# Transposes on TensorE in place of DMA transposes, and another order in the short chunks, in a one-core adaLN block with local attention and a gated MLP

## The chip, the cores and the metric

The kernel runs on one core of one Trainium2 chip. The metric is the device time of one execution in microseconds (us). "Before" is the median of three runs of the unchanged kernel; one execution of it was profiled.

## What is computed

The block takes 2048 tokens of 576 features in bf16. `mod` is six vectors of 576, made from a condition `c`.

```python
sa, ca, ga, sb, cb, gb = silu(c) @ w_mod          # six vectors of 576
h = layernorm(x) * (1 + ca) + sa                  # LN1 and its modulation
q, k, v = split(h @ wqkv)                         # 32 heads of 18 features
# each token attends to 8 tokens: itself and those 2, 4, ... 14 positions back
o = softmax(q . k_window / sqrt(18)) @ v_window
x = x + ga * (o @ wo)
h = layernorm(x) * (1 + cb) + sb                  # LN2 and its modulation
x = x + gb * (((h @ w_gate) * (h @ w_up)) @ w_down)   # 4608 hidden features
```

## The kernel before

**Chunks and passes.** The tokens are cut into ten chunks (`SIZES`): chunks 0 to 3 have 128 tokens ("short"), chunks 4 to 9 have 256. The MLP runs in seven passes over the weights: passes 0 to 3 take one short chunk each, pass 4 takes chunks 4 and 5 together, pass 5 takes 6 and 7, pass 6 takes 8 and 9. In a pass `gate_up` multiplies the normalized tokens with blocks of gate and up weights (L667 for the first 512 features, L676 for the last 64); ScalarE (ACT) copies the result out of PSUM (L684), and VectorE (DVE) multiplies gate by up (L685). After every 512 tokens `down` multiplies by `w_down` (L715) and writes the rows out. Gate and up weights come in blocks by DMA, during pass 0 from the queue of GpSimd (POOL), later from SyncE's (SP).

**Attention beside the MLP.** While the MLP of one pass runs, the attention of the next pass's chunks is prepared. `project(ci)` does LN1 of a chunk (`ln_rows`), turns the rows into feature-major form `hT`, and multiplies for q and k (L480), their last 64 features (`qkr`, L487) and v (L505). The v rows go to a buffer in DRAM (`vd`, L512), from which `vsh`, the windows of v, are read back (L522). `attend(ci)` forms the logits (L548), the softmax on DVE and ACT, the weighted sum over `vsh` (L606 to L609) that gives `o_sb`, turns that into `oT`, multiplies by `wo` (L623), adds to x, does LN2 into `o_sb`, and turns that into `h2T`, the input of the chunk's MLP pass.

**Order.** These two generators stop at labels (`hT`, `q0`, `v0`, `oT`, `wo0`, `h2T` and so on). `period(ci)` merges `project(ci + 1)` and `attend(ci)` by a table that gives each label a place between 0 and 1 in the period of the chunk, and `Pacer` lets a step go as the emitted MLP matmuls reach that place. There are three tables: `AT_SHORT` for chunks of 128, `AT_FIRST` for chunks 4 and 5, and `AT` for chunks 6 to 9. So the order of TensorE's (PE's) instructions is largely fixed by the tables. In passes 0 to 3 a scheduler also moves them; from pass 4 PE's order is as emitted. The setup before pass 0 is written out by hand.

**Turning.** Five feature tiles cover 576 features. The fifth has only 64, and they are wanted twice, on partitions 0 to 63 and again on 64 to 127, since L676 uses both halves of the array. So the rows `xn` and `o_sb` are 640 wide (`DP`), and `ln_rows` writes features 512 to 575 a second time into columns 576 to 639 (the second round of the loop at L385; ACT at L390 or DVE at L388). `turn` (L403 to L410) makes five 128x128 transposes on PE for each 128 tokens into two PSUM banks, and ACT and DVE bring them back with the modulation (`modulate`, L429 and L431), or ACT copies them for `oT` (L616, L617). For the chunks in `BY_DMA` (`hT` of 7, 8, 9; `oT` of 6 to 9; `h2T` of 4 and 6 to 9) `turn_by_dma` writes the rows to DRAM and reads them back with a DMA transpose, both from SP's queue (L414, L415), and POOL modulates in place (L420).

```python
        for m in range(n):
            for j in range(C // P):
                nc.tensor.transpose(banks[b][:, m, j * P:(j + 1) * P], src[:, j, (m0 + m) * P:(m0 + m + 1) * P], ident)
```

Of the kernel before, what the change touches and what calls it, by code (L numbers as in the profile page):

```python
# [16 lines left out]

P = 128
D = 576
DP = 640  # L20
KT = 5
H = 32
DH = 18
# [26 lines left out]
LOAD_X = {3: [6]}  # L50
LOAD_X_DOWN = {0: [7, 8], 1: [9]}

BY_DMA = dict(hT={7, 8, 9}, oT={6, 7, 8, 9}, h2T={4, 6, 7, 8, 9})

AT = dict(lg0=.06, lg1=.14, lgT=.19, hT=.31, q0=.37, q1=.41, k0=.45, k1=.49, qkr=.52, v0=.55, v1=.58,
          ws=.60, oT=.61, wo0=.66, wo1=.70, h2T=.86)

AT_FIRST = dict(AT, hT=.24, q0=.29, q1=.34, k0=.39, k1=.44, qkr=.48, v0=.52, v1=.57, ws=.64, oT=.66, wo0=.70, wo1=.74, h2T=.92)

AT_SHORT = dict(AT_FIRST, oT=.55, wo0=.60, h2T=.80)  # L60


@with_exitstack
def kernel(
# [41 lines left out]
    def hp():  # L106
        return tc.high_priority()
# [27 lines left out]
    xn = once.tile([P, CH // P, DP], BF, name="xn")  # L135
# [4 lines left out]
    o_sb = once.tile([P, CH // P, DP], BF, name="o_sb")  # L140
    oT = once.tile([P, KT, CH], BF, name="oT")
    vd = dramp.tile([HALO + S, D], BF, name="vd")
    turned = {k: dramp.tile([CH, DP], BF, name=f"{k}_d") for k in ("xn1", "o", "xn2")}

    nc.scalar.preload_act_table_set("natural_log_exp_and_others")

# [38 lines left out]
    nc.vector.memset(o_sb[:, :, D:], 0.0)  # L185

    def wm_tile():
        return sp.tile([P, KT, 2 * D], BF, name="wm", bufs=2)
# [175 lines left out]
    def ln_rows(src, into, j0=0, dve=False):  # L364

        ST = len(src)

        st = small.tile([P, CH // P, 14], F32, name="ln_stats", bufs=1)
        stats, mv = st[:, :, 0:12].rearrange("p j (a b) -> p j a b", a=2), st[:, :, 12:14]
        for j in range(ST):  # L370
            for hf in range(2):
                nc.vector.bn_stats(stats[:, j, hf, :], src[j][:, hf * 288:(hf + 1) * 288])  # L372
            nc.vector.bn_aggr(mv[:, j, :], stats[:, j, :, :].rearrange("p a b -> p (a b)"))
        rstd = small.tile([P, CH // P], F32, name="ln_rstd")
        nc.vector.tensor_scalar_add(rstd[:, 0:ST], mv[:, 0:ST, 1], EPS)  # L375
        nc.vector.tensor_scalar_mul(mv[:, 0:ST, 0], mv[:, 0:ST, 0], -1.0)
        yield
        nc.scalar.activation(rstd[:, 0:ST], rstd[:, 0:ST], ACTF.Ln)  # L378
        nc.scalar.activation(rstd[:, 0:ST], rstd[:, 0:ST], ACTF.Exp, scale=-0.5)
        if not dve:  # L380
            nmr = small.tile([P, CH // P], F32, name="ln_nmr")
            for j in range(ST):
                nc.scalar.activation(nmr[:, j:j + 1], mv[:, j, 0:1], ACTF.Identity, scale=rstd[:, j:j + 1])  # L383
        yield
        for d0, s0 in ((slice(0, D), 0), (slice(D, DP), D - 64)):  # L385
            for j in range(ST):
                if dve:
                    nc.vector.tensor_scalar(into[:, j0 + j, d0], src[j][:, s0:D], mv[:, j, 0:1], rstd[:, j:j + 1], ALU.add, ALU.mult)  # L388
                else:
                    nc.scalar.activation(into[:, j0 + j, d0], src[j][:, s0:], ACTF.Identity, bias=nmr[:, j:j + 1], scale=rstd[:, j:j + 1])  # L390

    def banks2(early, dt, name):

# [9 lines left out]
    def turn(src, C, early=False):  # L403

        banks = [b[:, 0:n * C].rearrange("p (m c) -> p m c", c=C) for b, n in zip(banks2(early, BF, "turn"), (3, 2))]
        for b, m0, n in ((0, 0, 3), (1, 3, 2)):
            for m in range(n):
                for j in range(C // P):
                    nc.tensor.transpose(banks[b][:, m, j * P:(j + 1) * P], src[:, j, (m0 + m) * P:(m0 + m + 1) * P], ident)
# [27 lines left out]
    def project(ci):  # L437
# [4 lines left out]
        for _ in ln_rows(x_tiles[ci], xn, j0):  # L442
            if ci == 1:
                yield "ln"
        h = hT[:, :, j0 * P:j0 * P + C]
        if ci in BY_DMA["hT"]:
            turn_by_dma(h, xn, "xn1")
            yield "hT"
            modulate_in_place(h, 0)
        else:  # L450
            yield "hT"
            banks = turn(xn[:, j0:, :], C, early=ci == 1)
            if ci < 2:
                yield "hTe"
            modulate(h, banks, 0, act_only=ci == 1)
# [68 lines left out]
    def attend(ci, dst):  # L524
# [76 lines left out]
        else:  # L601
            for j in range(ST):
# [10 lines left out]
            if ci not in BY_DMA["oT"]:  # L613
                banks = turn(o_sb, C)
        if ci not in BY_DMA["oT"]:
            (nc.vector.tensor_copy if ci == 0 else nc.scalar.copy)(oT[:, 0:3, 0:C], banks[0])  # L616
            nc.scalar.copy(oT[:, 3:5, 0:C], banks[1])  # L617
        for j in range(ST):
            yield f"wo{j}"
            pw = banks2(ci == 0, F32, "pw")  # L620
# [11 lines left out]

        for _ in ln_rows(x_t, o_sb, dve=ci == 0):
            pass
        if ci in BY_DMA["h2T"]:
            turn_by_dma(dst, o_sb, "xn2")
        yield "h2T"
        if ci in BY_DMA["h2T"]:
            modulate_in_place(dst, 2)
        else:  # L640
            modulate(dst, turn(o_sb, C), 2)

    def gate_up(pi, c0, C, h2, step):

# [4 lines left out]
        cs = slice(c0, c0 + C)  # L649
        ns = C / 2.4  # L650

        def tokens(rows, kt):
            return h2[rows, :, kt, :] if C > CH else h2[rows, c0 // CH, kt, c0 % CH:c0 % CH + C]

        def by_half(ap):
            return ap.rearrange("p (a c) -> p a c", c=CH) if C > CH else ap


        nf = 2 if C <= 256 else 1
        units = [(b, i) for b in ORDER[pi] for i in range(0, FB, nf)]  # L660
# [1 line left out]
        def main(u, first):  # L662
            (b, i), out = units[u], ps[u]
            for n in range(nf):
                for t in range(2):
                    for kt in range(KT - 1):
                        nc.tensor.matmul(by_half(out[:, t, n, 0:C]), lhsT=gu_blocks[b][0][:, kt, t, (i + n) * P:(i + n + 1) * P], rhs=tokens(slice(0, P), kt),  # L667
                                         start=(first and n == 0 and kt == 0), stop=(not first and kt == KT - 2), skip_group_check=True)
                step(8 * ns)

        def rem(u, first):
            (b, i), out = units[u], ps[u]
            for n in range(nf):
                for t in range(2):
                    rows = slice(64 * t, 64 * (t + 1))
                    nc.tensor.matmul(by_half(out[:, t, n, 0:C]), lhsT=gu_blocks[b][1][rows, (i + n) * P:(i + n + 1) * P], rhs=tokens(rows, KT - 1),  # L676
                                     start=(first and n == 0), stop=not first, skip_group_check=True)

        def evacuate(u):
# [52 lines left out]
    def attend_into_place(ci):  # L732
        di, c0 = home[ci]
        if di not in h2T:
            h2T[di] = h2p.tile([P, CM // CH, KT, CH], BF, name="h2T")
        return attend(ci, h2T[di][:, c0 // CH, :, c0 % CH:c0 % CH + SIZES[ci]])

    def period(ci):

        gens = {"a": project(ci + 1)} if ci + 1 < NCH else {}  # L740
        gens["b"] = attend_into_place(ci)
        at = AT_SHORT if SIZES[ci] == P else AT_FIRST if ci < 6 else AT
        nxt = {k: next(g) for k, g in gens.items()}
        while nxt:
            k = min(nxt, key=lambda k: at[nxt[k]])
            yield at[nxt[k]]
            nxt[k] = next(gens[k], None)
            if nxt[k] is None:
                del nxt[k]
# [121 lines left out]
```

## Time and profile before

| | |
|---|---|
| median of 3 runs | 582.46 us (582.19 to 582.83) |
| profiled execution, its own time | 582.19 us |
| its span | 580.5 us |
| PE busy | 564.4 us (97%), 5171 matmuls |
| DVE busy | 309.0 us (53%) |
| ACT busy | 258.6 us (45%) |
| POOL busy | 92.5 us (16%) |
| granted PE clock | 1.0 throughout |
| DMA | 84.33 MB, mean 145 GB/s |

The span runs from the first to the last instruction; the execution's own time is 1.7 us longer. A matmul's time in the profile (219 ns for one with 128 columns) holds its way through the array; how many of them PE does in a stretch is read from their starts.

### The profile page before, as it was taken

How to read it: one execution, taken by the hardware profiler on the slowest of the kernel's cores; microseconds unless marked ns; L12 is line 12 of the kernel's file. 1: busy time of each engine (PE TensorE's matmuls, PEld its weight loads, DVE VectorE, ACT ScalarE, POOL GpSimd, SP SyncE). 2: the span in 40 equal slices, each digit the busy share in tenths (PEclk: the TensorE clock that was granted, in tenths of full speed). 3: DMA queues.
4: the chain of work that ended last, by engine and by line, in shares of the span. 5: the costliest groups of instructions: out<-in, count | busy, mean ns of one | idle time of the engine just before them, and what ended most of it. 6: DMA issues, size and time to landing. Idle time of an engine off the chain costs nothing.

```text
span 580.5 us, 12340 instructions
## 1 busy us (share of the span) xinstructions
PE 564.4 (97%) x5171; PEld 368.8 (64%) x5171; DVE 309.0 (53%) x687; ACT 258.6 (45%) x475; POOL 92.5 (16%) x165
## 2 busy tenths in 40 slices
PE   7999999999999999999999999999999999999996
PEld 4577888878878764554458774554457754444675
DVE  5777686857868765845376525844374412222101
ACT  3465667575552245456542225455440225454200
POOL 4553201021113112011400231011200020000000
PEclk9999999999999999999999999999999999999999
DMA  8999763458751254477502542486302214550000
GB/s 291 273 355 341 251 201 115 134 184 269 248 184 44 75 189 113 127 245 218 136 1 77 194 103 93 118 251 219 95 1 56 67 39 144 155 163 1 1 21 20
DMA packets 68458, 84.33 MB, mean 145 GB/s; under 512 B 19618, under 2 KB 59506, under 8 KB 68402
## 3 DMA queue, kind: packets, MB, share of 16 engines
q1 hardware_dynamic: 56738, 45.86, 27.3%
q0 software_dynamic: 9104, 34.44, 17.9%
q10 hardware_dynamic: 2560, 3.25, 1.6%
q8 instruction: 40, 0.66, 0.5%
q14 instruction: 16, 0.13, 0.1%
HBM read 70.93 MB, written 8.67 MB: 137 GB/s over the span
## 4 chain that ended last, share of the span: by engine, by line
PE 79%; DMA 8%; ACT 5%; DVE 4%; issue 2%; POOL 1%; SPq 0%; ACTq 0%; POOLq 0%
PE pgu L667 38%; PE acc L715 22%; PE pgu L676 6%; PE pq L480 5%; DMA vd<-v_sb 3%; PE lgT L548 2%; DMA wd<-in_B_w_up_dram 2%; ACT gu L684 2%; DMA wqk<-in_A_wqkv_dram 2%; DMA wv<-in_A_wqkv_dram 2%; PE pwB L623 1%; PE pwA L623 1%; PE pvB L505 1%; PE pvA L505 1%; ACT o_sb L390 1%
## 5 line engine op out<-in xcount | busy, mean ns | idle before, releaser
L667 PE MATMUL pgu<-h2T,gm 128*128 128x512 bf16 (+1 forms) x1504 | 239.0, 311 | 0.6 <-ACT gu L684 0.3
L684 ACT CAST gu<-pgu 128x1024 bf16<-128x1024 f32 (+1 forms) x180 | 145.2, 843 | 122.2 <-PE pgu L676 97.7
L667 PEld LDWEIGHTS <-gm 128*128 128x128 bf16 x1504 | 118.4, 98 | 107.7 <-issue 15.7
L715 PE MATMUL acc<-wd,hh 128*128 128x288 bf16 x1152 | 146.5, 286 | 0.5 <-DVE y L721 0.5
L685 DVE TENSOR_TENSOR hh<-gu 128x512 bf16<-128x512 bf16 (+1 forms) x180 | 66.2, 371 | 144.9 <-ACT gu L684 144.0
L715 PEld LDWEIGHTS <-hh 128*128 128x128 bf16 x1152 | 112.3, 98 | 29.5 <-issue 1.2
L539 DVE TENSOR_TENSOR prod<-qT,kT 128x1280 bf16<-128x1280 bf16 (+1 forms) x80 | 46.8, 637 | 13.5 <-PE lgT L548 12.4
L522 POOL DMA_DIRECT2D vsh<-vd x30 | 22.6, 756 | 153.4 <-DMA vd<-v_sb 89.1
L721 DVE TENSOR_TENSOR y<-acc,gb_bc 128x576 bf16<-128x576 f32 (+1 forms) x17 | 12.3, 721 | 57.9 <-PE acc L715 57.9
L480 PE MATMUL pq<-hT,wqk 128*128 128x256 bf16 (+1 forms) x400 | 41.2, 251 | 0.8 <-DMA wqk<-in_A_wqkv_dram 0.8
L724 POOL DMA_DIRECT2D out_dram<-y x15 | 8.5, 566 | 208.1 <-DVE y L723 208.1
L606 DVE TENSOR_TENSOR vsh<-vsh,attn 128x2304 bf16<-128x2304 bf16 x30 | 39.9, 1351 | 0.2
L676 PE MATMUL pgu<-h2T,gr 64*128 64x512 bf16 (+1 forms) x376 | 37.0, 311 | 0.0
L480 PEld LDWEIGHTS <-wqk 128*128 128x128 bf16 x400 | 32.3, 98 | 6.8 <-DMA wqk<-in_A_wqkv_dram 1.5
L667 PE MATMUL pgu<-h2T,wd 128*128 128x128 bf16 x512 | 34.7, 219 | 1.4 <-DMA wd<-in_B_w_gate_dram 0.6
L667 PEld LDWEIGHTS <-wd 128*128 128x128 bf16 x512 | 30.4, 98 | 3.0 <-DMA wd<-in_B_w_up_dram 0.9
L372 DVE BATCH_NORM_STATS2 ln_stats<-x_t 128x6 f32<-128x288 bf16 x64 | 26.5, 447 | 7.4 <-ACT ln_nmr L383 5.3
L378 ACT ACTIVATE ln_rstd<-ln_rstd 128x2 f32<-128x2 f32 (+1 forms) x20 | 4.1, 203 | 53.5 <-DVE ln_rstd L375 53.4
L676 PEld LDWEIGHTS <-gr 64*128 64x128 bf16 x376 | 12.2, 94 | 18.9 <-issue 12.3
L420 POOL TENSOR_SCALAR h2T<-h2T,modc 128x256 bf16<-128x256 bf16 x25 | 14.7, 598 | 38.0 <-DMA h2T<-xn_d 38.0
L607 DVE TENSOR_TENSOR vsh<-vsh 128x2304 bf16<-128x2304 bf16 x15 | 20.2, 1349 | 0.0
L482 ACT CAST qT<-pq 128x512 bf16<-128x512 f32 (+1 forms) x20 | 10.1, 504 | 21.9 <-PE pq L480 21.9
(146 smaller groups left out, 483.3 us busy)
## 6 DMA issues: line engine op xcount, KB each, us to landing
vsh<-vd POOLq DMA_DIRECT2D x30, 576.0 KB, 6.3
gm<-in_B_w_gate_dram SPq DMA_DIRECT2D x24, 512.0 KB, 4.1
gm<-in_B_w_up_dram SPq DMA_DIRECT2D x24, 512.0 KB, 5.4
wd<-in_B_w_down_dram SPq DMA_DIRECT2D x4, 1152.0 KB, 7.0
gm<-in_B_w_gate_dram POOLq DMA_DIRECT2D x5, 512.0 KB, 11.7
gm<-in_B_w_up_dram POOLq DMA_DIRECT2D x5, 512.0 KB, 11.5
out_dram<-y POOLq DMA_DIRECT2D x15, 144.0 KB, 2.1
wd<-in_B_w_gate_dram POOLq DMA_DIRECT2D x4, 512.0 KB, 10.0
```

The costliest lines, as they stand in the source:

```text
L372: nc.vector.bn_stats(stats[:, j, hf, :], src[j][:, hf * 288:(hf + 1) * 288])
L420: nc.gpsimd.tensor_scalar(dst[:, m, :], dst[:, m, :], modc[:, vi + 1, m:m + 1], modc[:, vi, m:m + 1], ALU.mult, ALU.add)
L480: nc.tensor.matmul(pq[:, gi, 0:C], lhsT=wqk[:, kt, w0:w0 + P], rhs=h[:, kt, :], start=(kt == 0), stop=(kt == KT - 1))
L522: nc.gpsimd.dma_start(vsh[:].rearrange("p w d h -> p w (d h)"), src)
L539: nc.vector.tensor_tensor(prod[:, 0:nm, 0:C], qT[:, 0:nm, 0:C], kT[:, 0:nm, off:off + C], ALU.mult)
L606: nc.vector.tensor_tensor(vsh[:], vsh[:], attn[:, j, ws, None, :].to_broadcast([P, WG, DH, H]), ALU.mult)
L607: nc.vector.tensor_tensor(va[:], va[:], vb[:], ALU.add)
L667: nc.tensor.matmul(by_half(out[:, t, n, 0:C]), lhsT=gu_blocks[b][0][:, kt, t, (i + n) * P:(i + n + 1) * P], rhs=tokens(slice(0, P), kt), s ...
L676: nc.tensor.matmul(by_half(out[:, t, n, 0:C]), lhsT=gu_blocks[b][1][rows, (i + n) * P:(i + n + 1) * P], rhs=tokens(rows, KT - 1), start=(f ...
L684: nc.scalar.copy(g, ps[u][:, :, :, 0:C].rearrange("p t n c -> p n t c"))
L685: nc.vector.tensor_tensor(hh[:, fs, cs], g[:, :, 0, :], g[:, :, 1, :], ALU.mult)
L715: nc.tensor.matmul(acc[:, q, 0:288], lhsT=hh[:, f, j * P:(j + 1) * P], rhs=wd[:, f, q * 288:(q + 1) * 288], start=(f == 0), stop=(f == FT ...
```

## The change

- All chunks are turned on PE. `BY_DMA`, `turn_by_dma`, `modulate_in_place` and the three DRAM buffers go away. Twelve turns of 256 tokens are concerned: three of `hT`, four of `oT`, five of `h2T`.
- The rows are 576 wide. `ln_rows` no longer writes the last 64 features twice. `turn` makes the fifth tile of each 128 tokens by two transposes of 64 columns, one to the upper and one to the lower 64 partitions.
- `h2T` is one tile of 512 tokens in place of two halves of 256, so the matmuls of `gate_up` read their tokens as one run.
- The tables: chunks 6 to 9 now use what chunks 4 and 5 used (`hT` .24 for .31, q and k earlier by some .06 to .08, `oT` .66 for .61, `wo0` .70 for .66, `h2T` .92 for .86). For the short chunks `qkr` goes from .48 to .47, `oT` from .55 to .52, `wo0` from .60 to .59, `v0` from .52 to .66, `v1` from .57 to .72, `h2T` from .80 to .90.

```diff
-DP = 640
-BY_DMA = dict(hT={7, 8, 9}, oT={6, 7, 8, 9}, h2T={4, 6, 7, 8, 9})
-AT = dict(lg0=.06, lg1=.14, lgT=.19, hT=.31, q0=.37, q1=.41, k0=.45, k1=.49, qkr=.52, v0=.55, v1=.58,
-          ws=.60, oT=.61, wo0=.66, wo1=.70, h2T=.86)
-AT_FIRST = dict(AT, hT=.24, q0=.29, q1=.34, k0=.39, k1=.44, qkr=.48, v0=.52, v1=.57, ws=.64, oT=.66, wo0=.70, wo1=.74, h2T=.92)
-AT_SHORT = dict(AT_FIRST, oT=.55, wo0=.60, h2T=.80)
+AT = dict(lg0=.06, lg1=.14, lgT=.19, hT=.24, q0=.29, q1=.34, k0=.39, k1=.44, qkr=.48, v0=.52, v1=.57,
+          ws=.64, oT=.66, wo0=.70, wo1=.74, h2T=.92)
+AT_SHORT = dict(AT, qkr=.47, oT=.52, wo0=.59, v0=.66, v1=.72, ws=.51, h2T=.90)
...
-        for d0, s0 in ((slice(0, D), 0), (slice(D, DP), D - 64)):
-            for j in range(ST):
...
-                    nc.scalar.activation(into[:, j0 + j, d0], src[j][:, s0:], ACTF.Identity, bias=nmr[:, j:j + 1], scale=rstd[:, j:j + 1])
+        for j in range(ST):
...
+                nc.scalar.activation(into[:, j0 + j, :], src[j][:], ACTF.Identity, bias=nmr[:, j:j + 1], scale=rstd[:, j:j + 1])
...
-                    nc.tensor.transpose(banks[b][:, m, j * P:(j + 1) * P], src[:, j, (m0 + m) * P:(m0 + m + 1) * P], ident)
+                    out = banks[b][:, m, j * P:(j + 1) * P]
+                    if m0 + m < KT - 1:
+                        nc.tensor.transpose(out, src[:, j, (m0 + m) * P:(m0 + m + 1) * P], ident)
+                    else:
+                        for rows in (slice(0, 64), slice(64, P)):
+                            nc.tensor.transpose(out[rows], src[:, j, D - 64:D], ident)
...
-    def turn_by_dma(dst, src, key):
-        nc.sync.dma_start(turned[key][:].rearrange("(j p) n -> p j n", p=P), src[:])
-        nc.sync.dma_start_transpose(out=dst, in_=turned[key][:])
-    def modulate_in_place(dst, vi):
-        with hp():
-            for m in range(KT):
-                nc.gpsimd.tensor_scalar(dst[:, m, :], dst[:, m, :], modc[:, vi + 1, m:m + 1], modc[:, vi, m:m + 1], ALU.mult, ALU.add)
...
-        if ci in BY_DMA["hT"]:
-            turn_by_dma(h, xn, "xn1")
-            yield "hT"
-            modulate_in_place(h, 0)
-        else:
-            yield "hT"
+        yield "hT"
...
+        banks = turn(xn[:, j0:, :], C, early=ci == 1)
+        modulate(h, banks, 0, act_only=ci == 1)
...
-            if ci in BY_DMA["oT"]:
-                turn_by_dma(oT[:], o_sb, "o")
             yield "oT"
+            banks = turn(o_sb, C)
...
-        if ci in BY_DMA["h2T"]:
-            turn_by_dma(dst, o_sb, "xn2")
         yield "h2T"
-        if ci in BY_DMA["h2T"]:
-            modulate_in_place(dst, 2)
-        else:
-            modulate(dst, turn(o_sb, C), 2)
+        modulate(dst, turn(o_sb, C), 2)
...
-            h2T[di] = h2p.tile([P, CM // CH, KT, CH], BF, name="h2T")
+            h2T[di] = h2p.tile([P, KT, CM], BF, name="h2T")
...
-        at = AT_SHORT if SIZES[ci] == P else AT_FIRST if ci < 6 else AT
+        at = AT_SHORT if SIZES[ci] == P else AT
```

More of the change, by code (lines that the diff above doesn't have):

```diff
@@ L134 @@
     gb_bc = consts.tile([P, D], BF, name="gb_bc")
-    xn = once.tile([P, CH // P, DP], BF, name="xn")
+    xn = once.tile([P, CH // P, D], BF, name="xn")
     hT = once.tile([P, KT, CH], BF, name="hT")
@@ L139 @@
     v_sb = once.tile([P, D], BF, name="v_sb")
-    o_sb = once.tile([P, CH // P, DP], BF, name="o_sb")
+    o_sb = once.tile([P, CH // P, D], BF, name="o_sb")
     oT = once.tile([P, KT, CH], BF, name="oT")
     vd = dramp.tile([HALO + S, D], BF, name="vd")
-    turned = {k: dramp.tile([CH, DP], BF, name=f"{k}_d") for k in ("xn1", "o", "xn2")}
     nc.scalar.preload_act_table_set("natural_log_exp_and_others")
@@ L184 @@
         nc.vector.memset(t[64:, KT - 1, :], 0.0)
-    nc.vector.memset(o_sb[:, :, D:], 0.0)
     def wm_tile():
@@ L384, in ln_rows @@
         yield
-        for d0, s0 in ((slice(0, D), 0), (slice(D, DP), D - 64)):
-            for j in range(ST):
-                if dve:
-                    nc.vector.tensor_scalar(into[:, j0 + j, d0], src[j][:, s0:D], mv[:, j, 0:1], rstd[:, j:j + 1], ALU.add, ALU.mult)
-                else:
-                    nc.scalar.activation(into[:, j0 + j, d0], src[j][:, s0:], ACTF.Identity, bias=nmr[:, j:j + 1], scale=rstd[:, j:j + 1])
+        for j in range(ST):
+            if dve:
+                nc.vector.tensor_scalar(into[:, j0 + j, :], src[j][:], mv[:, j, 0:1], rstd[:, j:j + 1], ALU.add, ALU.mult)
+            else:
+                nc.scalar.activation(into[:, j0 + j, :], src[j][:], ACTF.Identity, bias=nmr[:, j:j + 1], scale=rstd[:, j:j + 1])
     def banks2(early, dt, name):
@@ L408, in turn @@
                 for j in range(C // P):
-                    nc.tensor.transpose(banks[b][:, m, j * P:(j + 1) * P], src[:, j, (m0 + m) * P:(m0 + m + 1) * P], ident)
-        return banks
-    def turn_by_dma(dst, src, key):
-        nc.sync.dma_start(turned[key][:].rearrange("(j p) n -> p j n", p=P), src[:])
-        nc.sync.dma_start_transpose(out=dst, in_=turned[key][:])
-    def modulate_in_place(dst, vi):
-        with hp():
-            for m in range(KT):
-                nc.gpsimd.tensor_scalar(dst[:, m, :], dst[:, m, :], modc[:, vi + 1, m:m + 1], modc[:, vi, m:m + 1], ALU.mult, ALU.add)
+                    out = banks[b][:, m, j * P:(j + 1) * P]
+                    if m0 + m < KT - 1:
+                        nc.tensor.transpose(out, src[:, j, (m0 + m) * P:(m0 + m + 1) * P], ident)
+                    else:
+                        for rows in (slice(0, 64), slice(64, P)):
+                            nc.tensor.transpose(out[rows], src[:, j, D - 64:D], ident)
+        return banks
     def modulate(dst, banks, vi, act_only=False):
@@ L444, in project @@
                 yield "ln"
+        yield "hT"
         h = hT[:, :, j0 * P:j0 * P + C]
-        if ci in BY_DMA["hT"]:
-            turn_by_dma(h, xn, "xn1")
-            yield "hT"
-            modulate_in_place(h, 0)
-        else:
-            yield "hT"
[L452 to L455, printed above, removed]
+        banks = turn(xn[:, j0:, :], C, early=ci == 1)
+        if ci < 2:
+            yield "hTe"
+        modulate(h, banks, 0, act_only=ci == 1)
         if ci == 0:
@@ L609, in attend @@
                 nc.vector.tensor_tensor(o_sb[:, j, 0:D].rearrange("p (d h) -> p d h", d=DH), va[:, 0], va[:, 1], ALU.add)
-            if ci in BY_DMA["oT"]:
-                turn_by_dma(oT[:], o_sb, "o")
             yield "oT"
[L613 to L617, printed above, removed]
+            banks = turn(o_sb, C)
+        (nc.vector.tensor_copy if ci == 0 else nc.scalar.copy)(oT[:, 0:3, 0:C], banks[0])
+        nc.scalar.copy(oT[:, 3:5, 0:C], banks[1])
         for j in range(ST):
@@ L634, in attend @@
             pass
-        if ci in BY_DMA["h2T"]:
-            turn_by_dma(dst, o_sb, "xn2")
         yield "h2T"
-        if ci in BY_DMA["h2T"]:
-            modulate_in_place(dst, 2)
-        else:
-            modulate(dst, turn(o_sb, C), 2)
+        modulate(dst, turn(o_sb, C), 2)
     def gate_up(pi, c0, C, h2, step):
@@ L650, in gate_up @@
         ns = C / 2.4
[L652 to L656, printed above, removed]
         nf = 2 if C <= 256 else 1
@@ L666, in main @@
                     for kt in range(KT - 1):
-                        nc.tensor.matmul(by_half(out[:, t, n, 0:C]), lhsT=gu_blocks[b][0][:, kt, t, (i + n) * P:(i + n + 1) * P], rhs=tokens(slice(0, P), kt),
+                        nc.tensor.matmul(out[:, t, n, 0:C], lhsT=gu_blocks[b][0][:, kt, t, (i + n) * P:(i + n + 1) * P], rhs=h2[:, kt, cs],
                                          start=(first and n == 0 and kt == 0), stop=(not first and kt == KT - 2), skip_group_check=True)
@@ L675, in rem @@
                     rows = slice(64 * t, 64 * (t + 1))
-                    nc.tensor.matmul(by_half(out[:, t, n, 0:C]), lhsT=gu_blocks[b][1][rows, (i + n) * P:(i + n + 1) * P], rhs=tokens(rows, KT - 1),
+                    nc.tensor.matmul(out[:, t, n, 0:C], lhsT=gu_blocks[b][1][rows, (i + n) * P:(i + n + 1) * P], rhs=h2[rows, KT - 1, cs],
                                      start=(first and n == 0), stop=not first, skip_group_check=True)
@@ L734, in attend_into_place @@
         if di not in h2T:
-            h2T[di] = h2p.tile([P, CM // CH, KT, CH], BF, name="h2T")
-        return attend(ci, h2T[di][:, c0 // CH, :, c0 % CH:c0 % CH + SIZES[ci]])
+            h2T[di] = h2p.tile([P, KT, CM], BF, name="h2T")
+        return attend(ci, h2T[di][:, :, c0:c0 + SIZES[ci]])
     def period(ci):
```

## The prediction

> **What bounds the kernel now.** I first cut the span into three stages, since 97% busy is a mean. Columns: stretch, length, then busy time of PE, weight loads, DVE, ACT, POOL, granted clock, DMA share, GB/s.
>
> ```profile
> 0.00:52.00 52.00, 45.66 (x622) 31.08 (x623) 36.60 (x101) 26.47 (x73) 26.39 (x51) 1.00 1.00 311
> 52.00:215.00 163.00, 157.65 (x2168) 133.24 (x2166) 116.83 (x286) 91.69 (x208) 24.90 (x45) 1.00 0.56 178
> 215.00:580.00 365.00, 361.12 (x2387) 204.48 (x2385) 155.59 (x300) 140.46 (x194) 41.18 (x71) 1.00 0.36 107
> ```
>
> Until 52 us the DMA engines are full and PE waits for weights. After 215 us PE is never idle (the missing 3.9 us lie at the end, after the last matmuls), while DMA is busy 36%, DVE 43%. There any work given to PE lengthens the span by its own length, and nothing taken from DMA or POOL shortens it. Between, PE loses something. I asked the waits what, for 52 to 135 us (the short chunks' passes), and then PE's timeline. Columns of the waits: who waits for whom, us in all, times, longest.
>
> ```profile
> PE turnA L409 <- ACT o_sb L390: 2.4, 3, 0.8
> PE pvB L505 <- ACT kT L490: 0.7, 2, 0.6
> ```
>
> PE's timeline (start, time, line, tiles, shape, count) at the first of them:
>
> ```profile
> 61.12 0.62 PE L667 MATMUL pgu<-h2T,gm 128*128 128x128 bf16 x8
> 62.54 0.34 PE L409 MATMUL turnA<-identw,o_sb 128*128 128x128 bf16 x3 [0.80 <-ACT o_sb L390]
> 62.72 0.22 PE L409 MATMUL turnB<-identw,o_sb 128*128 128x128 bf16 x1
> 62.77 0.94 PE L667 MATMUL pgu<-h2T,gm 128*128 128x128 bf16 x14
> 63.83 0.23 PE L409 MATMUL turnB<-identw,o_sb 128*128 128x128 bf16 x1
> ```
>
> and ACT's:
>
> ```profile
> 61.62 0.87 ACT L390 ACTIVATE o_sb<-x_t,ln_nmr,ln_rstd 128x576 bf16<-128x576 bf16 x1
> 63.33 0.45 ACT L390 ACTIVATE o_sb<-x_t,ln_nmr,ln_rstd 128x64 bf16<-128x64 bf16 x1
> ```
>
> PE reaches the turn of `h2T` before LN2's rows are written, and the fifth tile waits for the second copy of 64 features, which ACT does after two evacuations. Last, the price of a transpose, from starts:
>
> ```profile
> 158.23 1.07 PE L667 MATMUL pgu<-h2T,gm 128*128 128x128 bf16 x16
> 159.13 0.50 PE L409 MATMUL turnA<-identw,o_sb 128*128 128x128 bf16 x6
> 159.47 0.39 PE L409 MATMUL turnB<-identw,o_sb 128*128 128x128 bf16 x4
> 159.69 1.14 PE L715 MATMUL acc<-wd,hh 128*128 128x288 bf16 x8
> ```
>
> Ten transposes take 159.69 - 159.13 = 0.56 us, 56 ns each, with no loss before or after.
>
> **Price of the half transposes.** They write 64 of the 128 output partitions (128*64 in the profile). Only setup shows that shape: L598 makes tiles of 128 columns, and in two of its rounds the last tile has 64.
>
> ```profile
> 26.20 0.33 PE L598 MATMUL oTsA<-identw,vsh 128*128 128x128 bf16 x3
> 26.37 0.39 PE L598 MATMUL oTsB<-identw,vsh 128*128 128x128 bf16 x2
> 26.70 0.34 PE L598 MATMUL oTsA<-identw,vsh 128*128 128x128 bf16 x3
> 26.87 0.27 PE L598 MATMUL oTsB<-identw,vsh 128*128 128x128 bf16 x2
> 26.99 0.33 PE L598 MATMUL oTsA<-identw,vsh 128*128 128x128 bf16 x3
> ```
>
> The round with the 64-column tile (26.37) lasts 0.33 us to the next start, the one without (26.87) 0.12: going to the half shape and back costs about 0.22 us. Changes to L548 (128*32) and L676 (64*128) and back lose 0.1 us each way too. The two halves of a pair write different partitions; the only such pair, in setup, shows both starting together, 3 ns apart:
>
> ```profile
> L214 PE MATMUL pc<-identw,c_row x2: 210/211/212, 3.6 to 3.6; 9*64 9x9 bf16 x2
> ```
>
> So a pair costs one transpose, 0.06 us, if it behaves as that one; 0.11 if the halves queue. I take 0.06, the row with the same two halves.
>
> A rule of the Trainium skill speaks against this part: TensorEngine Tiling (Array Packing), Key Properties, says that a change of tiling mode drains TensorE. It gives no time; by the rule alone the term would be above zero, and L598 sizes it.
>
> **The sum.**
>
> 1. *Twelve turns of 256 tokens come to PE*: each 8 whole transposes x 0.056 + 2 pairs x 0.058 + 0.22 for the shape = 0.78 us; x12 = 9.4 us. One is in pass 3, the others after 215 us, where PE has no idle time to hide them: all on the path. Bounds: 12 x 10 x 0.056 = 6.7 us without switching, 10.7 us with queued halves.
>
> 2. *Seventeen turns that PE did already* get pairs for their fifth tile: +0.22 each. Three are in setup and one at 42 us among waits for weights, so hidden by DMA; 13 x 0.22 = 2.9 us (0 to 4).
>
> 3. *The short chunks.* The turn of `h2T` goes from .80 to .90; in the changed order 32 more short matmuls and the moved v projection stand before it. PE then arrives some 3 us later than the rows need (they end 4.6 us after `wo`; 7.4 us of PE work now lie between). So the losses go: start to start, 61.12 + 8 x 0.056 = 61.57, next start 62.54, 0.97 us; 62.77 + 14 x 0.056 = 63.55, next 63.83, 0.28 us; the same in all three passes: 3.75 us. v leaves its place behind `qkr`, where `pvB` waited for a PSUM bank (0.31, 0.72 and 0.32 us by starts): 1.35 us. Together 5.1. What is late next: in pass 0 the last weight block, issued from POOL at 51.82 and landing 11.5 us later (the page's median for that group), 63.3 us; its first use moves to about 62.8. That gives 0.5 back: 4.6 us. Bound above: all 17 losses over 0.14 us between 52 and 138 us make 7.35 us by starts; bound below 2.5, if ACT's evacuations take half.
>
> 4. *What the earlier `oT` and later v put at risk.* `o_sb` is written at 81.05 us in pass 1; PE's turn moves from 84.29 to some 81.5, margin 0.4 us; without it up to 0.5 us per pass. The later v writes `vd` from POOL's queue; in pass 0 that write waits behind the weight loads anyway (the `vsh` reads are issued at 64.28, as before), in pass 1 the reads move from 86.8 to about 91 and take up to 7.4 us, first use 105.2. Free. The turn of `h2T` ends 1.8 us (36 short matmuls and their losses) before pass 1 reads it; the modulation took 1.3 us from the last transpose (63.83) to its end (65.09). Free.
>
> 5. *Chunks 6 to 9 on PE.* `hT` follows the logits' transposes after 8 wide matmuls, 1.73 us; the bank it needs is held through two DVE operations of 0.69 us. In the short passes with 0.9 to 1.3 us between, such turns lost 0.31 to 0.34. I take 0.1 x 3 = 0.3 us; bounds 0 and 3.6 (0.3 for each of the twelve).
>
> 6. *Off the path.* ACT loses 31 copies x 0.43 = 13.3 us and gains 4 x 1.40 (`oT`) + 3 x 1.11 + 5 x 1.10 (modulation) = 14.4. DVE gains 8 x 3 x 0.40 = 9.7 us in 365 of which it works 156; POOL loses 40 x 0.6 us. SP loses 24 issues; PE waited for none of the landings behind them after 215 us. One run of 512 tokens or two of 256: by starts, matmuls of 128, 256 (L480, one run) and 512 columns (L667, two runs) come every 56, 109 and 216 ns, on one line, so nothing is to be gained. All zero; were ACT's new work late, PE would meet it through PSUM, which is in the bound of term 5.
>
> Sum: 9.4 + 2.9 - 4.6 + 0.3 = +8.0 us. The profiled execution took 582.19 us (span 580.5 and 1.7 around it); 590.2 us, or 590.4 from the median, which is 0.27 higher.
>
> VectorE: DVE Perf Modes, Rules for kernel authors, says to transpose 128x128 on TensorE where PSUM will do, and lists 390 ns there against 1309 by DMA. Here the turn by DMA costs the full engine nothing, and TensorE's takes 56 ns of it; at 390 ns, term 1 would be 12 x 10 x 0.39 = 47 us, an estimate from that page that no row supports.
>
> **Rivals.**
>
> *A. The short chunks pay for all of it (faster).* One mechanism: ACT, relieved of the row copies, stops holding PE in passes 0 to 2, so that all 17 losses go, and the half transposes hide their change of shape. 6.7 - 7.35 = -0.65, less another microsecond in pass 3 or setup: about 580.8 us. For it: two of the three kinds of loss end in ACT. Against: it wins only if the losses removed exceed 6.7 us without switching, 12.6 with it, and all that the stage shows is 7.35.
>
> *B. Changing shape is free (slower, small).* Terms 1 and 2 lose 25 x 0.22 = 5.5 us: 585 us. Against: L598, L548 and L676 all show it.
>
> *C. Turns wait for rows and banks.* PE takes its queue in order, so each turn that comes too early stops the MLP behind it. At the 0.5 us that the turn at 210 us lost (0.36 + 0.21 by starts), 12 turns give 6 us: 596 us. Against: in the long passes the tables leave microseconds between rows and turn.
>
> That the change doesn't do what it says is excluded: its instruction order has 167 more matmuls, 12 x 12 + 23 pairs' second halves.
>
> **How the numbers follow.** Forecast 586.5 to 594.5: 0.66. B, 583.8 to 586.5: 0.13. C, 594.5 to 599: 0.16. A: 0.05. Most of A is faster by over 0.2% (1.2 us, about what a measurement of this kernel can tell): 0.04; within 0.2%: 0.04, from the rest of A and the low end of B; slower: 0.92. The range 585 to 596 takes the forecast and half of B and C, 0.80.
>
> **What would show it.** Right: PE still without idle time after the short passes, and the turns of the long passes at about 0.78 us each by starts; no wait of `turnA` for `o_sb` in passes 0 to 2, and pass 3 beginning some 2 us sooner than now. Wrong: a turn of 0.56 us (B), waits before the turns of chunks 6 to 9 (C), or a first half shorter by more than 7 us (A).

## The result: 592.44 us, slower by 1.7%

The changed kernel took 592.44 us (median of four runs, 592.29 to 592.99), the kernel before 582.64 us (also four, 582.19 to 583.52): a ratio of 1.0168, 95% interval 1.015 to 1.0186. That is 9.8 us more; 8.0 were forecast. The profiled execution took 592.56 us, its span 590.9 us, 10.4 us more than the one of before. In what follows, lengths of stages are taken between PE's own landmarks (the first gate matmul of a pass, the first matmul of a `down`), one profiled execution for each kernel.

The three stages of the changed kernel (columns as before: stretch, length, busy time of PE, weight loads, DVE, ACT, POOL, then clock, DMA share, GB/s):

```profile
0.00:52.00 52.00, 47.16 (x639) 32.12 (x640) 36.18 (x99) 25.98 (x72) 26.86 (x51) 1.00 1.00 313
52.00:215.00 163.00, 158.01 (x2180) 133.09 (x2178) 116.69 (x290) 86.17 (x193) 21.39 (x38) 1.00 0.54 174
215.00:580.00 365.00, 365.00 (x2477) 207.04 (x2476) 160.85 (x319) 149.27 (x205) 21.35 (x36) 1.00 0.28 87
```

After 215 us PE is busy for all of 365.00 us and the DMA share fell from 0.36 to 0.28. What the DMA engines no longer do shortened nothing there, and what PE does more made the span longer. One of the turns, in PE's timeline:

```profile
260.47 0.50 PE L403 MATMUL turnA<-identw,o_sb 128*128 128x128 bf16 x6
260.80 0.27 PE L403 MATMUL turnB<-identw,o_sb 128*128 128x128 bf16 x2
261.01 0.30 PE L406 MATMUL turnB<-identw,o_sb 128*64 128x128 bf16 x4
261.24 1.04 PE L634 MATMUL pgu<-h2T,gm 128*128 128x512 bf16 x4
```

From the first transpose to the next gate matmul it takes 261.24 - 260.47 = 0.77 us; 0.78 were forecast. The two whole transposes at 260.80 take 0.21 us where two in a row would take 0.11: 0.10 us goes on entering the half shape. The four halves and the way out take 0.23. A turn of 128 tokens, which has one pair, takes 0.18 for the same (64.19 to 64.37 below), so a pair adds 0.057 us, as much as a whole transpose, and 0.12 us goes on leaving. The halves of a pair start 3 ns apart.

In the short passes the waits of `turnA` for `o_sb` and of `pvB` for `kT` are no longer listed, and others are (PE's waits from 52 to 135 us: who waits for whom, us in all, times, longest):

```profile
PE pgu L634 <- ACT gu L651: 1.8, 3, 0.9
PE pgu L634 <- DMA wd<-in_B_w_up_dram: 0.5, 1, 0.5
PE turnB L403 <- DVE dd L550: 0.2, 1, 0.2
```

By starts one loss ahead of a `pvB` is left, 0.30 us in pass 2 (118.67 to 119.10). PE at the first of the waits (start, time, line, tiles, count), and ACT in the same place:

```profile
60.51 0.51 PE L643 MATMUL pgu<-h2T,gr 64*128 64x128 bf16 x12
60.95 1.07 PE L634 MATMUL pgu<-h2T,gm 128*128 128x128 bf16 x16
62.53 1.50 PE L634 MATMUL pgu<-h2T,gm 128*128 128x128 bf16 x24 [0.51 <-ACT gu L651]
63.87 0.33 PE L403 MATMUL turnA<-identw,o_sb 128*128 128x128 bf16 x3
64.04 0.22 PE L403 MATMUL turnB<-identw,o_sb 128*128 128x128 bf16 x1
64.19 0.25 PE L406 MATMUL turnB<-identw,o_sb 128*64 128x128 bf16 x2
64.37 0.62 PE L634 MATMUL pgu<-h2T,gm 128*128 128x128 bf16 x8
```

```profile
60.11 0.87 ACT L382 ACTIVATE o_sb<-x_t,ln_nmr,ln_rstd 128x576 bf16<-128x576 bf16 x1
61.25 0.20 ACT L371 ACTIVATE ln_rstd<-ln_rstd 128x1 f32<-128x1 f32 x1 [0.27 <-DVE ln_rstd L368]
61.72 0.29 ACT L376 ACTIVATE ln_nmr<-ln_stats,ln_rstd 128x1 f32<-128x1 f32 x1
61.92 1.05 ACT L651 CAST gu<-pgu 128x512 bf16<-128x512 f32 x2
```

The turn of `h2T` (63.87) runs without waiting. But PE stands before it: 16 matmuls that need 0.89 us last from 60.95 to 62.53, a loss of 0.69 us. They are ready and have no PSUM bank, for the copies that would free one (61.92) stand in ACT's queue behind the rows of LN2 and behind LN1 of a later chunk, which itself waits for DVE. The like happens at 92.81 (0.64 us lost) and 121.18 (1.04), where the rows of a later LN1 themselves stand ahead of the copies on ACT.

Where the time went, against the kernel before (us, from the landmarks; the forecast's terms are laid to the same stretches, with 2, 6, 2 and 3 of term 2's 13 turns from pass 0 to the `down` of pass 3):

| stretch | forecast | changed kernel | e2: order alone | e3: whole transposes | e4: two v buffers |
|---|---|---|---|---|---|
| setup | 0 | +0.71 | -0.28 | -0.62 | -0.18 |
| pass 0 | -0.62 | -1.39 | -0.41 | -0.77 | -0.76 |
| passes 1 and 2 | -2.22 | -1.44 | -2.22 | -2.24 | -1.55 |
| pass 3, gate and up | +0.44 | +1.66 | +1.98 | +1.33 | +0.44 |
| `down` of pass 3 | +1.44 | +1.61 | +0.07 | +1.22 | +0.67 |
| pass 4 to the last `down` | +8.9 | +8.82 | 0 | +6.25 | +8.83 |
| last `down` to the end | 0 | +0.40 | 0 | +0.42 | +0.41 |
| sum | +7.9 | +10.37 | -0.87 | +5.58 | +7.86 |

Setup differs by such amounts from one profiled execution to the next (34.8 to 36.1 us among these five kernels), whatever the change; without it the sum is +9.7, close to the 9.8 of the medians. Pass 0, in which PE still waits for weights until 54 us, varies too: the kernel before, e1, e8, e11 and e12 have the same order of instructions there, and it took them 31.56, 30.72, 30.61, 31.50 and 30.78 us, so the kernel before was caught at the long end and differences of up to 1 us in this row say nothing. Passes 1 and 2 took all five 62.08 to 62.10 us; there a difference of 0.1 us can be read.

### The profile page after: what moved, and what is told of

The parts are those of the page before. It is cut to its first block, busy times and chain, and to the rows that moved or that the text cites. A ratio compares the mean times of both kernels' runs of the same rounds, so it can differ in the third digit from the quotient of the medians.

```text
span 590.9 us, 12596 instructions
## 1 busy us (share of the span) xinstructions
PE 576.3 (98%) x5338; PEld 376.7 (64%) x5338; DVE 315.3 (53%) x709; ACT 261.4 (44%) x468; POOL 69.6 (12%) x125
## 4 chain that ended last, share of the span: by engine, by line
PE 83%; DMA 7%; DVE 5%; ACT 3%; issue 1%; POOL 0%; ACTq 0%; DVEq 0%
PE pgu L634 39%; PE acc L682 22%; PE pgu L643 6%; PE pq L462 5%; DMA wd<-in_B_w_up_dram 4%; DMA wm<-in_w_mod_dram 4%; PE lgT L530 2%; DVE ln_stats L365 2%; PE pwA L601 1%; PE pwB L601 1%; PE warm L265 1%; PE pvA L487 1%; PE turnA L403 1%; PE pvB L487 1%; DVE y L606 1%
## 5 line engine op out<-in xcount | busy, mean ns | idle before, releaser
L601 PE MATMUL pwA<-wo,oT 128*128 128x288 bf16 x75 | 19.1, 286 | 0.6 <-ACT oT L594 0.6
L487 PEld LDWEIGHTS <-hT 128*128 128x128 bf16 x160 | 15.0, 98 | 7.0 <-DMA wv<-in_A_wqkv_dram 1.9
```

The costliest lines, as they stand in the source:

```text
L487: nc.tensor.matmul(pv[q][:, 0:288], lhsT=h[:, kt, j * P:(j + 1) * P], rhs=wv[:, kt, q * 288:(q + 1) * 288], start=(kt == 0), stop=(kt == K ...
L601: nc.tensor.matmul(pw[q][:, 0:288], lhsT=oT[:, m, j * P:(j + 1) * P], rhs=wo[:, m, q * 288:(q + 1) * 288], start=(m == 0), stop=(m == KT - 1))
```

## Experiments

Twelve kernels ran, each in five rounds beside the kernel before. They are told by the question they answer. What is "before" in a ratio is that kernel's median in the same job: 581.7 for e1, e2, e3 and e5, 582.0 for the others up to e10, 581.9 for the last two.

### What do twelve turns cost?

**e1**: before, with every turn on PE and all else left (row copies, whole transposes, old tables).

```diff
-BY_DMA = dict(hT={7, 8, 9}, oT={6, 7, 8, 9}, h2T={4, 6, 7, 8, 9})
+BY_DMA = dict(hT=set(), oT=set(), h2T=set())
```

> The kernel before, with all its twelve DMA turns made on PE; tables, row copies and the full shape of every transpose stay as they were. Theory (after 215 us every matmul start on PE is on the path, a whole transpose costs 56 ns): 12 turns x 10 x 0.056 = 6.7 us, so 589.3 us against 582.6. Rival (the turns also wait, for rows or for PSUM banks, some 0.5 us each): 595 us. Rival (the DMA turns had delayed something, so part comes back): under 587 us.

Measured: 590.57 us, ratio 1.0152 (1.0139 to 1.0165). Giving the turns to PE makes nearly all of the loss. The eleven turns from pass 4 on cost 7.13 us: 11 x 0.56 = 6.2, and 1.0 more. PE's timeline has that 1.0 in one place, at chunk 8's first q projection (ACT first, then PE):

```profile
301.56 1.01 ACT L684 CAST gu<-pgu 128x1024 bf16<-128x1024 f32 x1 [0.94 <-DVE hh L685]
302.47 1.03 ACT L431 ACTIVATE hT<-turnB,modc 128x256 bf16<-128x256 bf16 x2
```

```profile
303.55 0.49 PE L480 MATMUL pq<-hT,wqk 128*128 128x256 bf16 x2 [0.17 <-ACT hT L431]
304.42 0.81 PE L480 MATMUL pq<-hT,wqk 128*128 128x256 bf16 x6 [0.39 <-DVE hT L429]
```

By starts PE lost 0.34 us before the first of these lines and 0.66 before the second: with the old table the projection follows the turn too closely for the modulation, of which DVE does its share only from 302.99 us on, behind a product of the weighted sum (L606), and ACT its own from 302.47, behind the copy shown.

**e11** and **e12** ask whether this turn alone is behind the 1.0: e11 puts only the three `hT` turns on PE, e12 all but chunk 8's `hT`.

```diff
-BY_DMA = dict(hT={7, 8, 9}, oT={6, 7, 8, 9}, h2T={4, 6, 7, 8, 9})
+BY_DMA = dict(hT=set(), oT={6, 7, 8, 9}, h2T={4, 6, 7, 8, 9})   # e11
+BY_DMA = dict(hT={8}, oT=set(), h2T=set())                      # e12
```

> The kernel before, with the three hT turns of chunks 7, 8 and 9 as ten whole transposes on PE, all else as it was: the nine other turns stay with the DMA, and so does the old table. Two things are asked. First, e1's turns cost 1.0 us more than 11 x 0.56, and PE's timeline put it at the turn of chunk 8's hT (0.34 and 0.66 us before the first q projection). Theory: hT is the turn that is late in the old table, so the three cost 3 x 0.56 + 1.0 = 2.7 us by the segments; rival: the twelve together load ACT and DVE, and three alone cost 1.7 us. Second, what lies between the last block of down and the end of the span is 0.40 us longer in all six kernels without DMA transposes (40.37 us for 39.97), and in these six alone the profile shows one packet of the instruction queue within the last 1 us. If any DMA transpose in the program prevents it, 39.97 here; if it depends on how many, 40.37 may come.

> The same the other way round: the kernel before with only chunk 8's hT turned by DMA, eleven turns on PE. Theory: e1's extra 1.0 us was at this one turn, so it goes with the turn's own 0.56, and the profile's sum falls from e1's +7.45 to +5.9 us (588.0 us by the medians); rival, the eleven others carry it: +6.9 us. The tail from the last block of down: 39.97 if one DMA transpose in the program is enough to avoid the late instruction packet, 40.37 if not.

Measured: e11 584.67 us, 1.0045 (1.0027 to 1.0063), +2.67 us from pass 4 to the last `down`, with the same two losses of 0.34 and 0.66 us; e12 588.39 us, 1.011 (1.0091 to 1.0129), +6.0 us in all, of which +5.58 from pass 4 to the last `down`, 10 x 0.56. The theory held in both. This is rival C's mechanism, met once in twelve turns, and only with the old table. The changed kernel shows no loss there: its table leaves 2.74 us of PE's work between the last transpose of chunk 8's `hT` and the projection, where e1 had 2.0, its three `hT` turns take 0.83 us in place of 0.77, and PE has no listed wait from 215 to 560 us.

### What does the half shape cost?

**e3**: the changed kernel with 640-wide rows, the second row copy and whole transposes put back.

```diff
-                    if m0 + m < KT - 1:
-                        nc.tensor.transpose(out, src[:, j, (m0 + m) * P:(m0 + m + 1) * P], ident)
-                    else:
-                        for rows in (slice(0, 64), slice(64, P)):
-                            nc.tensor.transpose(out[rows], src[:, j, D - 64:D], ident)
+                    nc.tensor.transpose(out, src[:, j, (m0 + m) * P:(m0 + m + 1) * P], ident)
...
-        for j in range(ST):
+        for d0, s0 in ((slice(0, D), 0), (slice(D, DP), D - 64)):
+            for j in range(ST):
```

> The changed kernel with the second copy of the last 64 features back: rows 640 wide, ln_rows writes the features twice, turn makes five whole transposes for each 128 tokens. Tables and PE turns stay as changed. Theory (the half transposes cost 0.22 us per turn for the change of shape, 25 turns on the path): 5.5 us less, 586.9 us. Rival (the change of shape hides, and the 31 copies cost ACT time that PE meets): 592 us or more.

Measured: 588.67 us, 1.0122 (1.0107 to 1.0137): some 3 to 4 us less than the changed kernel, where 5.5 were expected. In the long passes a turn costs 6.25/11 = 0.57 us here and 8.82/11 = 0.80 in the changed kernel, so the shape costs 0.23 us per turn, as L598 had shown in setup. The 0.57 holds the new layout of `h2T` too, and e1's 0.56 the old one, so the layout brings nothing that can be seen. In passes 1 and 2, where six turns should have saved 1.3 us, e3 is ahead by 0.8 only. TensorEngine Tiling (Array Packing) of the Trainium skill, Key Properties, says that a change of mode drains TensorE; the long passes agree in that each change costs time, 0.10 us in and 0.12 out.

**e5**: the kernel before, with halves in place of the second row copy on the turns that PE already made.

```diff
-        for d0, s0 in ((slice(0, D), 0), (slice(D, DP), D - 64)):
+        for d0, s0 in ((slice(0, D), 0), (slice(D, DP), D - 64))[0:1 + twice]:
```

(`twice` holds for the chunks that the DMA turns; the halves in `turn` are those of the change.)

> The kernel before, with half transposes and no second copy for the turns that PE made already; DMA turns keep their copies, all tables stay. Theory: 13 x 0.22 = 2.9 us more, less up to 0.8 us where the fifth tile of h2T no longer waits for its copy in passes 0 to 2: 584.7 to 585.5 us. Rival (no cost of shape): 582 us.

Measured: 583.38 us, 1.0032 (1.0021 to 1.0044): less than expected. From the landmarks, pass 1 grew by 0.49 us and pass 2 by 0.29, three turns each, where 0.66 was priced; pass 3's gate stretch grew by 0.45 (two turns, 0.44 priced), and its `down` not at all (-0.04; three turns, 0.66 priced). The 0.78 of passes 1 and 2 is what e3 found there. So the shape costs its full price where PE alone is late, and a part of it comes back elsewhere. In the short passes that part comes from the row copies that ACT is spared: the second loss of the old order, 0.28 us ahead of the fifth tile of `h2T`, isn't there in e5, and the loss at the end of pass 1 is 0.64 us in the changed kernel, 0.97 in e3. Which wait gives it back in the `down` is not shown; the 0.3 us that PE had waited there for `v_sb` is no longer listed.

### What did the order of the short chunks bring?

**e2**: before, with the new short table alone.

```diff
-AT_SHORT = dict(AT_FIRST, oT=.55, wo0=.60, h2T=.80)
+AT_SHORT = dict(AT_FIRST, qkr=.47, oT=.52, wo0=.59, v0=.66, v1=.72, ws=.51, h2T=.90)
```

> The kernel before, with only the new table for the short chunks; DMA turns, row copies and the tables of the long chunks stay. Theory (the new order takes away 4.8 us of PE's losses in passes 0 to 2, and about 2 us of that is lost again at the end of pass 3, where the second v of chunk 4 waits for the write of the first to land beside the down weights): 579.8 us, pass 3 beginning some 4.8 us sooner. Rival (nothing is given back): 577.8 us. Rival (the new order itself saves nothing, the gain came from ACT's dropped copies): 582.6 us.

Measured: 581.36 us, 0.9994 (0.9985 to 1.0002): a miss. Passes 0 to 2 are shorter by 2.63 us, not 4.8, and of these only the 2.22 in passes 1 and 2 are clear of pass 0's spread. The gate stretch of pass 3 is longer by 1.98, as the expectation had it, though the v block is one of chunk 5. ACT in the changed kernel shows where:

```profile
152.71 0.33 ACTq L494 DMA_DIRECT2D vd<-v_sb  x1
153.19 0.59 ACT L651 CAST gu<-pgu 128x512 bf16<-128x512 f32 x1 [0.51 <-DVE hh L652]
157.44 0.40 ACT L491 CAST v_sb<-pvA 128x288 bf16<-128x288 f32 x1 [3.67 <-PE pgu L634]
```

and PE's waits from 135 to 220 us:

```profile
PE pwA L601 <- ACT oT L594: 0.6, 1, 0.6
PE acc L682 <- ACT gu L651: 0.5, 1, 0.5
PE turnA L403 <- ACT v_sb L491: 0.5, 1, 0.5
```

ACT idles for 3.67 us ahead of the second v evacuation of chunk 5. The profile names PE's `pgu` as the releaser, which is no input of this copy. In the kernel before, the same copy waits for 1.34 us, and there the profile names the write:

```profile
157.25 0.40 ACT L509 CAST v_sb<-pvA 128x288 bf16<-128x288 f32 x1 [1.34 <-DMA vd<-v_sb]
```

In the changed kernel `v_sb` is one buffer as well, and its first write to `vd`, issued at 152.71, lands at 157.37; ACT goes on at 157.44. The write runs beside the last two blocks of down weights, issued at 145.68 and 146.90, which land at 153.73 and 156.94. In the kernel before it was issued 1.9 us later, at 154.60, and landed at the same time, 157.18: the earlier start gained nothing, for those weights land no earlier either, though issued 1.9 us sooner. In the new order the last v reads of chunk 4 come 8.4 us later (129.25 and 129.99, in place of 120.85 and 121.59) and take up to 7.2 us beside the weight loads; e7 asks whether that is why the weights come no sooner. Behind the evacuation wait the copies of `gu` and `oT`, and for them PE, in four places.

**e4** tests this on the changed kernel, with a second buffer (two small softmax tiles go to one buffer to make room):

```diff
-                vt = v0 if ci == 0 else v_sb
+                vt = v0 if ci == 0 else once.tile([P, D], BF, name="v_sb", bufs=2)
```

> The changed kernel with two buffers for v_sb instead of one (to make room, the softmax's two small row tiles mx and ssum have one buffer each). Theory (at the end of pass 3 ACT holds its queue for the single v_sb until the first v write has landed, and PE waits behind ACT): 1.2 to 1.9 us less, 590.5 to 591.2 us, the step from pass 3 to its down back to some 0.6 us. Rival (PE waits there for the down weights or for something else): 592.4 us.

Measured: 589.94 us, 1.0139 (1.0125 to 1.0154), 1.7 us less by the ratios. The gate stretch of pass 3 falls to +0.44, the price of its two turns in the half shape and nothing else, its `down` from +1.61 to +0.67, and ACT's evacuation comes at 154.16, without a wait for the write, which lands at 155.80:

```profile
154.16 0.40 ACT L490 CAST v_sb<-pvA 128x288 bf16<-128x288 f32 x1 [0.75 <-PE pvA L486]
```

**e7** put v of the last short period alone back to its old place.

```diff
-        at = AT_SHORT if SIZES[ci] == P else AT
+        at = (dict(AT_SHORT, v0=.52, v1=.57) if ci == 3 else AT_SHORT) if SIZES[ci] == P else AT
```

> The changed kernel with v0 and v1 back at .52 and .57 in the period of chunk 3 alone, where chunk 4 is projected. Theory (the reads of v for chunk 4, moved from 121 to 129 us, fall among the loads of the down weights and hold them up, and these hold up the v write at the end of pass 3): the reads clear the loads, and about 1 us comes back: 591.4 us. Rival (the collision does not matter; only the single v_sb does): 592.4 us.

Measured: 591.65 us, 1.0172 (1.0159 to 1.0185): by the ratio no change against the changed kernel. The trace is clearer. Chunk 4's last v reads are issued at 118.91 and 119.65 us and have landed at 126.98, before the loads of the down weights begin (129.91). The last two of these, issued within 0.1 us of where the changed kernel issues them, land at 151.58 and 154.86, 2.1 us sooner, and the gate stretch of pass 3 is 0.85 us shorter. So the later reads do hold up the weights. Passes 1 and 2 are as long as in the changed kernel; pass 0 was 0.5 longer, which is within its spread. In e4, too, the last weights land 2.6 us sooner (154.38), and chunk 4's second v write is issued at 121.67 in place of 124.66: e4 takes away both the wait for the buffer and a part of the collision.

**e8** is the kernel before with the two buffers of e4 and no more.

> The kernel before with two buffers for v_sb, nothing else (mx and ssum share a small tile). Theory (before, PE met the wait for v_sb at the end of pass 3 hardly at all: 0.3 us): 582.3 us. Rival (the second buffer is worth as much by itself): 581 us.

Measured: 581.01 us, 0.9982 (0.9974 to 0.9991): the single buffer cost the old order about 1 us too (0.5 to 1.5 by the interval). The landmarks show 0.65 of it, in the `down` of pass 3, where PE had waited 0.3 us for `v_sb`; passes 1 and 2 are unchanged to 0.01 us, so the single buffer of the softmax tiles costs nothing there. The rival in the expectation was right.

**e6** joins e2 and e8: the order with the buffer that it needs, and no new work on PE.

> The kernel before with the new table for the short chunks and two buffers for v_sb (mx and ssum share one small tile to make room); DMA turns and row copies stay. Theory: the 4.8 us of passes 0 to 2 without the loss at the end of pass 3: 577.5 to 578.5 us. Rival (the loss there is set by the landing of the down weights): 580 us.

Measured: 579.2 us (578.99 to 581.8, six runs), 0.9961 (0.9947 to 0.9976): faster than both kernels, than the one before by 0.4%, about 1 us less than expected. Its profiled execution (581.8) is the slowest of the six, with pass 0 starting at 40.1 us, so its setup and pass 0 are not compared. That microsecond is looked for next.

**e9** holds LN1 of chunks 3 and 4 back in e6, behind the last gate-times-up product of the pass before, by a DVE copy of one element, so that ACT does the evacuations first. **e10** is the same edit on e4.

```diff
+        if behind is not None:
+            nc.vector.tensor_copy(rstd[0:1, 0:1], behind)
```

> This is e6 (before, with the new table of the short chunks and two buffers for v_sb) with one small DVE copy of a single element put in front of LN1's small operations of chunks 3 and 4, so that they can't begin before the gate-times-up product of the preceding pass is written. In the new order ACT does LN1's rstd and nmr while the gate and up evacuations stand behind them, and PE loses 0.97 and 0.87 us before the next pass in e6's passes 1 and 2 (0.68 in pass 0). Theory: ACT's in-order queue, with LN1's small operations ahead of the evacuations, makes that loss; then the losses at the ends of the passes that the edit reaches fall by 0.7 to 1.0 us each and the time is about 577.8 us beside 579.2 for e6, 1.4 less. Rival: the row activation of LN2 (0.87 us, still ahead of the evacuations) makes it, or the loss only moves to the turn of hT, which now gets its rows later: 579.2 us, no change.

> The same edit on e4 (the changed kernel with two buffers for v_sb). Theory, ACT's queue order makes the 0.64 to 1.04 us that PE loses at the ends of the short passes: 589.9 falls to about 588.5 us. Rival, the row activation makes it or the loss moves to the turn of hT: 589.9 us.

Measured: e9 578.65 us, 0.9942 (0.9922 to 0.9961); e10 589.55 us, 1.0133 (1.0106 to 1.0159). Both lie between theory and rival, and their intervals reach over those of e6 and e4, so the times don't tell. The traces do. In e9 ACT now goes from the rows straight to the evacuations, and PE runs through (first PE, then ACT):

```profile
61.10 2.41 PE L668 MATMUL pgu<-h2T,gm 128*128 128x128 bf16 x40
```

```profile
60.26 1.20 ACT L391 ACTIVATE o_sb<-x_t,ln_nmr,ln_rstd 128x576 bf16<-128x576 bf16 x2
61.36 1.57 ACT L685 CAST gu<-pgu 128x512 bf16<-128x512 f32 x3
```

Forty matmuls of 56 ns need 2.24 us and take 2.25 to the next start (63.35): the loss at the end of pass 0 is gone, and at the end of pass 1 as well. So ACT's order made those losses, with the row activation still in its place. But chunk 4's LN1, held back, now stands in the way in pass 2, where PE lost 1.13 us by starts on the way to this line, because `lgs` (97.86) is behind the held-back rows of `xn`:

```profile
98.28 0.28 PE L565 MATMUL lg<-identw,lgs 128*128 128x128 bf16 x2 [0.81 <-ACT lgs L552]
```

The sum of setup and pass 0 is 0.74 us shorter in e9 than in e2, about as much as that sum varies by itself; pass 1 is 0.9 shorter than in e6, pass 2 0.95 longer. In e10 the three steps against e4 are -0.62, -0.63 and +0.58. Holding chunk 3 alone was not tried.

## Why the prediction was right, and where its terms were off

The forecast mechanism, its sign and the range held, and its signs of being right came: no wait listed in the long passes, turns of 0.77 to 0.83 us there, no wait of `turnA` for `o_sb` in passes 0 to 2, pass 3 beginning 2.1 us sooner. 590.4 was 2 us too low. By the landmarks 1.2 us of that lie in the gate stretch of pass 3 and 0.4 at the end; that passes 0 to 2 together come out at -2.83 for -2.84 is luck, as point 3 shows.

1. *Twelve turns* (term 1): right. Eleven cost 8.82 us with term 5 in it, 8.9 forecast; each about 0.80 for 0.78, since PE had no idle time for any of it.
2. *The shape on old turns* (term 2): right per turn where PE alone is late (0.44 for two in pass 3's gate stretch, by e4), too high in passes 1 and 2. There six turns should have added 1.3 us, and the changed kernel is only 0.8 behind e3. The term priced the new shape without what ACT gives back by not copying rows; term 6 had called those copies worth nothing.
3. *The short chunks* (term 3): mis-sized. The named losses did go, the 0.97, the 0.28 and `pvB`'s, of which 0.30 us in pass 2 stayed. What is late next was looked for only in the last weight block of pass 0, for which PE never waited (its one wait for weights after 52 us is the 0.5 that ends at 54.06, 0.34 at the same block before). ACT's in-order queue took another 0.64 to 1.04 us in each pass. In passes 1 and 2 the order alone brings 2.2 us, where 3.5 was forecast (2 x 1.25 + 0.72 + 0.32). A part of this error is made up there by that of term 2: -1.44 us for -2.22. The rest is made up in pass 0, whose length in the one profile of the kernel before was at the long end of its spread.
4. *v later is free* (term 4): wrong, the main miss. The step counted POOL's reads, their landing and the first use of `vsh`, in passes 0 and 1. It left out that chunk 4's reads, in pass 2, move into the loads of the down weights and hold them up by 2.1 us (e7), that chunk 5's v write goes out into these weights, and that on ACT the evacuation of the next v block waits for it. In the gate stretch of pass 3 that is about 1.2 us in the changed kernel (e4 against it) and 2.0 in e2 (e6 against it). In the `down` e4 takes away another 0.9 us, but of a like loss the old order had 0.65 already (e8).
5. *Turn waits* (term 5): 0.3 forecast; no wait is listed, and the three `hT` turns took 0.06 us longer each than the others. What it stands for was there in e1, at 1.0 us for one turn.
6. *Off the path* (term 6): right after pass 3. The end adds 0.40 us that no step had.

Rival A fell with the first half: all of its losses were not to be had, since ACT, relieved of the copies, is held up by something else. B is excluded by e3. The part of A that holds is e6 and e9: the order does pay, once `v_sb` has two buffers and the turns stay where they cost PE nothing.

## What to carry to other kernels

Here the transfers that hid beside a full engine cost it nothing, slow as they were; work moved from it to that engine is paid in full, here 0.57 us a turn and 0.80 with the change of shape. When a step is moved, follow it through every queue that it uses and look for its single buffers: the step that reuses the buffer waits for the DMA that empties it, and the in-order engine makes everything behind it wait. When a stall is removed, read what stands next in the queue of the engine that was late, not only whether the named wait is met. And before a stretch is compared between two profiles, see how much it varies among kernels that do the same there: pass 0 here varies by 1 us, passes 1 and 2 by 0.02.

## Not expected of the hardware

- ACT, DVE and POOL keep their order strictly, as the Trainium skill says (Perfetto Trace Analysis, Tensor Engine Instruction); the size of it was not expected: three of LN1's smallest operations in the wrong place (61.25 to 61.92) cost PE 0.7 us, and an evacuation that waits for a DMA cost it 1.2 in one stretch.
- Leaving the half shape takes slightly longer (0.12 us) than entering it (0.10), and the two halves of a pair cost together what one transpose does (0.057 us, from turns with one and with two pairs).
- From the first matmul of the last `down` to the end, the seven kernels with at most one DMA transpose (the changed one, e1, e3, e4, e7, e10, e12) take 40.27 to 40.39 us, the seven others 39.86 to 39.97. In the last 3 us of the seven the DMA view has a packet that the others lack, after the last rows are written:

```profile
q14 instruction: 1, 0.01, 0.7%
```

A turn on PE alone doesn't bring it: e11, with three, has none. One DMA transpose in e12 doesn't prevent it. Where it comes from, and whether it makes the 0.40 us, was not tried.
